# High rows of a feed-forward product eight steps behind its low rows, and a new order in VectorE's list of deferred work

## The chip, the core and the metric

The kernel runs on one core of one Trainium2 chip. Its engines are TensorE (PE in the profile; PEld is its loading of weights), VectorE (DVE), ScalarE (ACT), GpSimd (POOL) and SyncE (SP), which here only issues transfers. Each works through its own row of instructions in the order of the program, and they wait for each other by semaphores. The metric is the time of one execution in microseconds (us); lower is better.

## The reference

The input x has 2048 rows of 512 values in float32. Two branches are computed from it and mixed by a gate of one number for each row.

```python
g = _sigmoid((x * gate_w).sum(-1, keepdims=True))
# a: 32 query heads of 16 columns, one key and one value head for all of them
q = (x @ wq).reshape(B, S, H, Dh).transpose(0, 2, 1, 3); k = x @ wk; v = x @ wv
p = _softmax(jnp.einsum("bhqd,bkd->bhqk", q, k) * Dh ** -0.5, axis=-1)
a = jnp.einsum("bhqk,bkd->bhqd", p, v).transpose(0, 2, 1, 3).reshape(B, S, 512) @ wo
# b: a feed-forward product with 1792 hidden columns
b = (_silu(x @ w_gate) * (x @ w_up)) @ w_down
return g * a + (1 - g) * b
```

## The kernel before

**Two kinds of work share TensorE.** Attention is cut into units: one head and 128 keys. A unit's scores for all 2048 queries fill two tiles `pss` of 128x1024 (L658), ScalarE turns them into `pt` by an exponential (L666), and four matmuls multiply `pt` by the values into `po` (L678, "the mix"; a block's four units make sixteen, which the profile counts as 32). The feed-forward work is a list of jobs. A gate job or an up job multiplies one chunk of 512 rows of x with 128 columns of `w_gate` or `w_up` in 12 matmuls; a down job multiplies finished hidden columns with `w_down` in 12 or 15. Every operand is kept as a high and a low float32r part (`xh`, `xl`), and three products of the parts stand for one.

**Blocks.** After a beginning, the loop runs blocks of four units (`block`, L709). A block's order is the string `STEPS`: eight S, each one score tile, and sixteen F, each one step of feed-forward work; then the mix of four units. I call the time from the start of one block's mix to the start of the next one's a period.

**Low and high rows.** TensorE takes a feed-forward matmul as two halves of 64 rows that run side by side. In a step, `Halves.step` (L377) issues one matmul of the low rows of one job and one of the high rows of another, older one. The high rows of a job may begin when `LAG` counts have passed since its low rows ended; a step counts 1, a score tile 1 and the mix 16. VectorE's one-element memset `sign` (L401) stands between the two halves of a job as a tick. Both halves add up in one bank of PSUM, and there are three such banks (`ps_f`, tiles `pf`). When the high rows end, VectorE empties the bank (`EVAC`): `hs<-pf` (L265) for a gate, the product `ht<-ht,pf` (L292) or `ht<-hs,pf` (L294) for an up, `acc` (L327, L329) for a down. `SLACK = 7` counts later the bank counts as free and the next low rows may be placed in it; on the chip their first matmul waits for that copy. Where a score tile that VectorE must help with follows within two places, the emptying is held back until that tile has been issued (`HOLD`), so it stands behind VectorE's copy `pt<-pss` (L662): for three tiles of a block VectorE copies one half of the scores out, and ScalarE works on that half in place later.

**VectorE's deferred list.** The gate needs silu, built from a tanh on ScalarE (L274, issued at the end of the block, behind its exponentials) and VectorE's `ht<-ht,hs` (L282, "the gate's product"). L282 goes into the list `DEFER`; so does, once the up job has ended, the pair that splits the finished hidden column, `hh<-ht` (L106) and `hl<-ht,hh` (L107), "the casts". If an up job ends before its L282 has been issued, `up` issues it on the spot, straight ahead of L292. If an up job ends in the same block as its gate, ahead of the tanh, the kernel multiplies first (L294), runs the tanh in place (L278) and defers L296 instead of L282. A second list, `LATER`, holds the six pieces of the normalization of a finished head: a shuffle (L696), four reciprocals (L687) and a product with its stores (L690), "the norms". At the end of a block, L740 to L745 issue up to two norms and then entries of `DEFER`, each with a cost, until the budget of 3.2 is used up or the head of the list doesn't fit. The mix is issued behind that and keeps TensorE busy meanwhile.

**The end.** Jobs that don't fit into the blocks are done with all 128 rows behind the last mix (`whole`, L355), and then the attention's output product (`finish`). GpSimd splits the weights (L106, L107 with `wgh`, `wdl` and so on) in that part as everywhere.

Of the kernel before, what the change touches and what calls it, by code (L numbers as in the profile page):

```python
# [36 lines left out]
ORDER = (0, 1, 2, 3)  # L37
GROUPS = ((0, 1, 2, 3, 4), (5, 6, 7, 8, 9), (10, 11, 12, 13))
SLACK = 7
LAG = 6  # L40
LONG = 8
GAP = 36
WARM = 30
# [19 lines left out]
def tile_gated_mix(ctx, tc, x, wq, wk, wv, wo, w_gate, w_up, w_down, gate_w, out):  # L63
# [41 lines left out]
    def split(hi, lo, src, eng=nc.gpsimd, eng_hi=nc.vector):  # L105
        eng_hi.tensor_copy(hi, src)  # L106
        eng.tensor_tensor(lo, src, hi.bitcast(F32), ALU.subtract)  # L107


    def three(a, b, sa, sb):  # L110
        return [(a[0][sa], b[0][sb]), (a[0][sa], b[1][sb]), (a[1][sa], b[0][sb])]
# [10 lines left out]
    ACTS, DEFER, LOADS, HOLD, EVAC = [], [], [], [], []  # L122

    def run(queue, n):
        for _ in range(min(n, len(queue))):
            queue.pop(0)()
# [16 lines left out]
    def load_w(nm, n):  # L143
        if n < NCH * NF:
            fs = slice(n % NF * P, (n % NF + 1) * P)
            if nm == "d":
                W[nm, n] = load_split(w_down[fs, :], "wd", 5)
            else:
                W[nm, n] = load_split({"g": wg_v, "u": wu_v}[nm][:, :, fs], "w" + nm, 2)
# [102 lines left out]
    def gate_up(n, c):  # L252
        t = []

        def project(nm):
            def terms():
                r = []
                for k in range(KD):
                    r += three(W[nm, n], XC[c], (slice(None), k), (slice(None), k))
                return r  # L260
            return terms

        def gate(ps):
            g = wp.tile([P, CH], F32, name="hs", bufs=2)
            nc.vector.tensor_copy(g, ps)  # L265

            t.append(wp.tile([P, CH], F32, name="ht", bufs=2))

            t.append(g)
            assert n < 2 or n - 2 in HT  # L270

            def tanh():
                if len(t) == 2:
                    nc.scalar.activation(t[0], g, AF.Tanh, scale=0.5)  # L274
                    DEFER.append((0.7, silu))
                    t.append(silu)
                else:
                    nc.scalar.activation(g, g, AF.Tanh, scale=0.5)  # L278

            def silu():  # L280
                if len(t) == 3:
                    nc.vector.scalar_tensor_tensor(t[0], t[0], 1.0, g, op0=ALU.add, op1=ALU.mult)  # L282
                    t.append(None)

            ACTS.append(tanh)

        def up(ps):
            hh = wp.tile([P, CH], F32R, name="hh", bufs=7)
            hl = wp.tile([P, CH], F32R, name="hl", bufs=7)
            if len(t) > 2:  # L290
                t[2]()
                nc.vector.tensor_tensor(t[0], t[0], ps, ALU.mult)  # L292
            else:
                nc.vector.tensor_tensor(t[0], t[1], ps, ALU.mult)  # L294
                t.append(lambda: None)
                DEFER.append((0.7, lambda: nc.vector.scalar_tensor_tensor(t[0], t[1], 1.0, t[0], op0=ALU.add, op1=ALU.mult)))  # L296

            def cast():
                split(hh, hl, t[0], nc.vector)
                HT[n] = (hh, hl)  # L300

            DEFER.append((1.2, cast))

        r = []
        for nm, end in (("g", gate), ("u", up)):
            r.append(Job(3 * KD, lambda nm=nm: (nm, n) in W and c in XC, project(nm), end))
            r[-1].after.append(lambda nm=nm: load_w(nm, n + 2))
        return r
# [67 lines left out]
    class Halves:  # L376
# [6 lines left out]
        def step(self, more):  # L383
# [3 lines left out]
            if not self.low and more and JOBS and JOBS[0].ready() and self.free and min(self.free) <= self.clock:  # L387
                self.free.remove(min(self.free))
                self.low = [JOBS.pop(0), 0]
            if not self.high and self.wait and self.wait[0][1] + LAG <= self.clock:  # L390
                self.high = [self.wait.pop(0)[0], 0]
# [241 lines left out]
    PO, LATER = [], []  # L633
    hp = tc.alloc_tile_pool(name="hp", bufs=2)
    with tc.tile_pool(name="bpool", bufs=2) as bp:
# [29 lines left out]
        def exps(pt, ps, other=None, w=slice(None)):  # L665
            ins = nc.scalar.activation(pt[:, w], ps[:, w], AF.Exp, scale=SCALE)  # L666
            if other is not None:
                tc.declare_no_dep(getattr(ins, "ins", ins), getattr(other, "ins", other), reason="another bank")

        def mix(u):  # L670
            h, kt = divmod(u, NT)
            pt = PT.pop(u)
            if kt == 0:
                run(COPY, 1)
                PO[:] = [ps_o.tile([P, CH], F32, name="po")]
            po = PO[0]
            for c in range(NCH):
                nc.tensor.matmul(po[c * 2 * DH:(c + 1) * 2 * DH, :], vaug[:, kt, :], pt[:, c * CH:(c + 1) * CH],  # L678
                                 start=(kt == 0), stop=(kt == NT - 1))
            if kt == NT - 1:  # L680

                osb = hp.tile([P, CH], F32, name="osb")
                rsb = hp.tile([P, CH], F32, name="rsb", bufs=1)

                def invert(i):
                    w = slice(i * P, (i + 1) * P)
                    nc.vector.reciprocal(rsb[:, w], rsb[:, w])  # L687

                def store():
                    nc.vector.tensor_tensor(osb, osb, rsb, ALU.mult)  # L690
                    for c in range(NCH):
                        nc.sync.dma_start(o_d[h * DH:(h + 1) * DH, c * CH:(c + 1) * CH],
                                          osb[c * 2 * DH:c * 2 * DH + DH, :])

                COPY.append(lambda: nc.vector.tensor_copy(osb, po))
                LATER.extend([(0.8, lambda: nc.vector.stream_shuffle(rsb, osb, [DH] * 2 * DH))] +  # L696
                             [(1.0, lambda i=i: invert(i)) for i in range(TC)] + [(0.8, store)])
# [5 lines left out]
        def feed(k, more=True):  # L703
            for _ in range(k):
                if JOBS and more or halves.busy():
                    halves.step(more)

        def block(k, first, last, steps, kinds, order):
            more = k < NB - STOP  # L709
            tiles = [(u, j) for u in range(first, last) for j in range(2)]  # L710
            order = list(order)
            made = []

            def emit():
                while order and order[0] != "|" and int(order[0][0]) < len(made):
                    i, how = int(order[0][0]), order.pop(0)[1]
                    pt, ps, other = made[i]
                    if how == "s":
                        exps(pt, pt, w=slice(CH, None))
                    else:  # L720
                        exps(pt, ps, other, slice(0, CH) if kinds[i] == "H" else slice(None))

            for i, what in enumerate(steps):
                if what == "F":
                    if "S" in steps[i + 1:i + 3] and kinds[len(made):len(made) + 1] == "H":
                        HOLD.append(i)
                    feed(1, more)
                    HOLD.clear()
                elif len(made) < len(tiles):
                    made.append(score(*tiles[len(made)], kinds[len(made)] == "H"))  # L730
                    emit()
                    run(EVAC, len(EVAC))
                if len(made) > 4:
                    run(COPY, 1)
            if order:
                order.pop(0)
            run(ACTS, len(ACTS))
            emit()
            assert not order and len(made) == len(tiles)
            left = BUDGET  # L740
            for queue, n in ((LATER, 2), (DEFER, len(DEFER))):
                while n and queue and queue[0][0] <= left:
                    cost, f = queue.pop(0)
                    left, n = left - cost, n - 1
                    f()  # L745
            for u in range(BLOCK * k, BLOCK * (k + 1)):
                mix(u)
            halves.clock += 2 * LONG
# [7 lines left out]
        with tc.manual_schedule():  # L756
# [25 lines left out]
            for k in range(2 * BEGIN // BLOCK, NB):  # L782
                u = BLOCK * k
                if k == 2 * BEGIN // BLOCK:
                    n = u + 6 - (u + 1)
# [129 lines left out]
```

## Time and profile before

| | |
|---|---|
| median of three runs | 1369.03 us (1368.62 to 1370.0) |
| the profiled execution, its own time | 1366.99 us |
| its span, from the first to the last instruction | 1364.9 us |
| granted TensorE clock, mean | 0.999 |
| busy share: TensorE, VectorE, ScalarE, GpSimd | 98%, 53%, 78%, 29% |

In the views quoted below, a row of a timeline gives the start in the span, the time, engine, line and operation, and in brackets how long the engine had been idle and what ended that. A row of the waits gives who waited for whom, total us, number and longest. A row of windows gives the stretch, its length, and the busy us of PE, PEld, DVE, ACT and POOL with instructions in brackets, the granted clock and the transfers. TensorE's busy share hides short waits, since matmuls overlap; the lengths of the periods don't.

### The profile page before, as it was taken

The numbers are of one execution on the slowest core, as the hardware profiler recorded it, in microseconds if no ns is written. First come the engines' busy times: TensorE is split into PE (matmuls) and PEld (weight loads), VectorE is DVE, ScalarE is ACT, GpSimd is POOL, SyncE is SP. The second block draws the span as 40 slices with busy tenths as digits, with TensorE's granted clock in tenths as the row PEclk, the third lists the DMA queues.
The fourth block names the chain that finished last, engine by engine and source line by source line (L and its number), as shares of the span: only waits on it lengthen the run. The fifth ranks groups of instructions, "written<-read, shape, count | busy, mean of one in ns | idle before, by whom it ended". The sixth has DMA issues, their size and how long they took to land. (4 is left out here: it accounts for less than half of the span.)

```text
span 1364.9 us, 26750 instructions
## 1 busy us (share of the span) xinstructions
PE 1332.3 (98%) x10755; PEld 767.4 (56%) x10755; DVE 722.6 (53%) x1222; ACT 1061.2 (78%) x1463; POOL 390.6 (29%) x408
## 2 busy tenths in 40 slices
PE   9999999999999999999999999999999999999997
PEld 7654555555555555555555555555555555555576
DVE  5554555455545456556455555456464566465432
ACT  4578888888888888888888888888888888888500
POOL 6140321052221232232041151232131331053353
PEclk9999999999999999999999999999999999999999
DMA  8455311131241221121151130231221221132154
GB/s 273 144 178 193 81 43 29 27 102 43 62 125 36 80 78 34 53 68 51 36 144 36 60 95 25 59 82 36 59 69 34 89 66 34 35 96 59 36 166 141
DMA packets 101489, 107.79 MB, mean 79 GB/s; under 512 B 9968, under 2 KB 69616, under 8 KB 99696
## 3 DMA queue, kind: packets, MB, share of 16 engines
q1 hardware_dynamic: 99632, 105.81, 27.0%
q8 instruction: 88, 1.44, 0.5%
q10 hardware_dynamic: 1728, 0.20, 0.1%
q14 instruction: 41, 0.34, 0.1%
HBM read 76.09 MB, written 29.36 MB: 77 GB/s over the span
## 5 line engine op out<-in xcount | busy, mean ns | idle before, releaser
L666 ACT ACTIVATE pt<-pss 128x1024 f32<-128x1024 f32 (+1 forms) x1024 | 841.1, 875 | 200.7 <-PE pss L658 170.4
L678 PE MATMUL po<-pt,vaug 128*32 128x512 f32 x4096 | 467.6, 595 | 0.0
L662 DVE COPY pt<-pss 128x512 f32<-128x512 f32 x354 | 244.6, 692 | 372.4 <-PE pss L658 332.8
L658 PE MATMUL pss<-qs,ks 64*128 64x512 f32 x2048 | 397.2, 415 | 2.0 <-ACT pt L666 1.1
L658 PEld LDWEIGHTS pss<-qs,ks 64*128 64x128 f32 x2048 | 192.4, 184 | 215.4 <-ACT pt L666 133.7
L678 PEld LDWEIGHTS po<-pt,vaug 128*32 128x32 f32 x4096 | 119.2, 109 | 261.5 <-issue 255.8
L666 ACT ACTIVATE pt<-pt 128x512 f32<-128x512 f32 x354 | 195.7, 620 | 0.0
L175 PE MATMUL pf<-xh,wgh 64*128 64x512 f32 (+1 forms) x444 | 165.7, 393 | 8.4 <-DVE sign L401 7.8
L175 PE MATMUL pf<-xh,wuh 64*128 64x512 f32 (+1 forms) x440 | 163.6, 393 | 4.0 <-DVE sign L401 3.2
L175 PE MATMUL pf<-xh,wgl 64*128 64x512 f32 (+1 forms) x444 | 165.5, 394 | 0.0
L175 PE MATMUL pf<-xl,wgh 64*128 64x512 f32 (+1 forms) x444 | 165.4, 390 | 0.0
L175 PE MATMUL pf<-xh,wul 64*128 64x512 f32 (+1 forms) x440 | 163.8, 394 | 0.0
L175 PE MATMUL pf<-wdh,hh 64*128 64x512 f32 (+1 forms) x427 | 154.6, 392 | 5.4 <-DVE sign L401 5.1
L175 PE MATMUL pf<-xl,wuh 64*128 64x512 f32 (+1 forms) x440 | 159.8, 390 | 0.0
L175 PE MATMUL pf<-wdl,hh 64*128 64x512 f32 (+1 forms) x427 | 153.5, 391 | 2.5 <-POOL wdl L107 2.5
L175 PE MATMUL pf<-wdh,hl 64*128 64x512 f32 (+1 forms) x427 | 155.7, 392 | 0.0
L106 POOL CAST wgh<-wraw 128x512 fp32r<-128x512 f32 x56 | 35.5, 634 | 402.6 <-PE pf L175 321.0
L106 POOL CAST wuh<-wraw 128x512 fp32r<-128x512 f32 x56 | 35.5, 634 | 323.4 <-PE pf L175 284.1
L687 DVE RECIPROCAL rsb<-rsb 128x128 f32<-128x128 f32 x128 | 117.0, 935 | 6.2 <-issue 4.5
L175 PEld LDWEIGHTS pf<-xh,wgh 64*128 64x128 f32 (+1 forms) x444 | 80.3, 185 | 19.5 <-issue 9.2
L175 PEld LDWEIGHTS pf<-xh,wuh 64*128 64x128 f32 (+1 forms) x440 | 79.6, 185 | 15.3 <-issue 6.2
L175 PEld LDWEIGHTS pf<-wdh,hh 64*128 64x128 f32 (+1 forms) x427 | 78.4, 185 | 15.7 <-DVE sign L401 7.5
(157 smaller groups left out, 1580.3 us busy)
## 6 DMA issues: line engine op xcount, KB each, us to landing
wraw<-in_B_w_gate_dram SPq DMA_DIRECT2D x56, 256.0 KB
wraw<-in_B_w_up_dram SPq DMA_DIRECT2D x56, 256.0 KB
wraw<-in_B_w_down_dram SPq DMA_DIRECT2D x56, 256.0 KB
qs<-q_d SPq DMA_DIRECT2D x62, 192.0 KB
q_d<-hl SPq DMA_DIRECT2D x18, 256.0 KB
q_d<-hh SPq DMA_DIRECT2D x18, 256.0 KB
o_d<-osb SPq DMA_DIRECT2D x128, 32.0 KB
a_d<-acc SPq DMA_DIRECT2D x4, 1024.0 KB
```

The source lines that it names most:

```text
L106: eng_hi.tensor_copy(hi, src)
L175: ins = nc.tensor.matmul(self.ps, a, b, start=(i == 0 and not half), stop=(last and half != 0))
L658: nc.tensor.matmul(ps[:, b * CH:(b + 1) * CH], ks[rows, kt * P:(kt + 1) * P], QS[h][rows, j, :], start=True, stop=True)
L662: other = nc.vector.tensor_copy(pt[:, CH:], ps[:, CH:]) if half else None
L666: ins = nc.scalar.activation(pt[:, w], ps[:, w], AF.Exp, scale=SCALE)
L678: nc.tensor.matmul(po[c * 2 * DH:(c + 1) * 2 * DH, :], vaug[:, kt, :], pt[:, c * CH:(c + 1) * CH], start=(kt == 0), stop=(kt == NT - 1))
L687: nc.vector.reciprocal(rsb[:, w], rsb[:, w])
```

## The change

`LAG` goes from 6 to 8, so the high rows of a job begin two counts later. The gate's product L282 goes to the head of `DEFER` and no longer to its end, so it stands ahead of the casts of the job before. With two or more entries in `DEFER`, a block issues one norm and not two. An assertion checks that `LATER` is empty when a new head's norms are added; it adds no instruction. From L695 on, line numbers grow by one.

```diff
-LAG = 6
+LAG = 8
...
                     nc.scalar.activation(t[0], g, AF.Tanh, scale=0.5)
-                    DEFER.append((0.7, silu))
+                    DEFER.insert(0, (0.7, silu))
...
+                assert not LATER
                 COPY.append(lambda: nc.vector.tensor_copy(osb, po))
...
             left = BUDGET
-            for queue, n in ((LATER, 2), (DEFER, len(DEFER))):
+            for queue, n in ((LATER, 1 if len(DEFER) > 1 else 2), (DEFER, len(DEFER))):
                 while n and queue and queue[0][0] <= left:
                     cost, f = queue.pop(0)
                     left, n = left - cost, n - 1
                     f()
```

Two places show what moves. The first is VectorE's row around one gate and its up job, from the emptying of the gate's bank (`hs<-pf`) to the tick behind the up job's product (`ht<-ht,pf`); `rsb` belongs to the norms, `pt<-pss` is the copy of scores. Before, about 617 to 626 us into the span:

```order
L265 COPY hs<-pf 128x512
L687 RECIPROCAL rsb<-rsb 128x128 x2
L106 CAST hh<-ht 128x512
L107 TENSOR_TENSOR hl<-ht,hh 128x512
L662 COPY pt<-pss 128x512
L401 MEMSET sign 1x1
L662 COPY pt<-pss 128x512 x2
L282 SCALAR_TENSOR_TENSOR ht<-ht,hs 128x512
L292 TENSOR_TENSOR ht<-ht,pf 128x512
L401 MEMSET sign 1x1
```

The same gate and up job in the changed kernel:

```order
L265 COPY hs<-pf 128x512
L687 RECIPROCAL rsb<-rsb 128x128
L282 SCALAR_TENSOR_TENSOR ht<-ht,hs 128x512
L106 CAST hh<-ht 128x512
L107 TENSOR_TENSOR hl<-ht,hh 128x512
L662 COPY pt<-pss 128x512
L401 MEMSET sign 1x1
L662 COPY pt<-pss 128x512 x2
L292 TENSOR_TENSOR ht<-ht,pf 128x512
L401 MEMSET sign 1x1
```

The gate's product has moved from directly ahead of L292, behind two copies of scores, to the end of the block before, ahead of the casts and of the next block's first copy.

The second place is TensorE's row in a block, with tile numbers: each `pf` number is one job in one bank. Before, in the same block, from the first high row of a new job (`pf_6978`) to the first low row of the next one (`pf_7126`), which takes the bank of `pf_6884`; that one's last high row stands two rows ahead of this piece, and its emptying is held back behind the score tile in the second row:

```order
L175 MATMUL pf_6978<-xh_230,wuh_6860 128x512
L658 MATMUL pss_7096<-qs_6482,ks_78 128x512 x2
L175 MATMUL pf_7068<-xh_230,wgl_6912 128x512
L175 MATMUL pf_6978<-xl_231,wuh_6860 128x512
L175 MATMUL pf_7068<-xh_230,wgh_6911 128x512
L175 MATMUL pf_6978<-xh_230,wul_6861 128x512
L658 MATMUL pss_7114<-qs_6482,ks_78 128x512 x2
L175 MATMUL pf_7068<-xl_231,wgh_6911 128x512
L175 MATMUL pf_6978<-xh_230,wuh_6860 128x512
L175 MATMUL pf_7068<-xh_230,wgl_6912 128x512
L175 MATMUL pf_6978<-xl_231,wuh_6860 128x512
L175 MATMUL pf_7126<-xh_230,wuh_7016 128x512
```

A block of the changed kernel, from the row behind the last high row of `pf_7707`; its emptying is issued at once, ahead of the score tile in the first row:

```order
L658 MATMUL pss_7942<-qs_7370,ks_78 128x512 x2
L175 MATMUL pf_7902<-xh_230,wuh_7392 128x512
L175 MATMUL pf_7801<-xh_230,wgh_7294 128x512
L175 MATMUL pf_7902<-xl_231,wuh_7392 128x512
L175 MATMUL pf_7801<-xl_231,wgh_7294 128x512
L175 MATMUL pf_7902<-xh_230,wul_7393 128x512
L175 MATMUL pf_7801<-xh_230,wgl_7295 128x512
L658 MATMUL pss_7953<-qs_7370,ks_78 128x512 x2
L175 MATMUL pf_7902<-xh_230,wuh_7392 128x512
L175 MATMUL pf_7801<-xh_230,wgh_7294 128x512
L175 MATMUL pf_7902<-xl_231,wuh_7392 128x512
L175 MATMUL pf_7801<-xl_231,wgh_7294 128x512
```

The first low row in `pf_7707`'s bank comes another score tile and two rows later. From a bank's last high row to its next user there were five steps and two score tiles; here there are six and three, and the copy is not held back. Of the emptyings in the 118 blocks ahead of the last one, 61 of 149 were held back before, and 28 of 148 are now.

## Prediction

> **What bounds the kernel now.** I read the page first, then who waits on TensorE, then windows of one period each, then the timeline of single waits.
>
> ```profile
> span 1364.9 us, 26750 instructions
> PE 1332.3 (98%) x10755; PEld 767.4 (56%) x10755; DVE 722.6 (53%) x1222; ACT 1061.2 (78%) x1463; POOL 390.6 (29%) x408
> ```
>
> TensorE is busy for 98%, so only its waits and its number of steps can move the time. Who waits on TensorE:
>
> ```profile
> engine line waited for: us in total, times, longest us
> PE pf L175 <- DVE sign L401: 16.1, 22, 1.8
> PE pf L175 <- POOL wdl L107: 2.5, 2, 1.4
> PE pss L658 <- ACT pt L666: 1.1, 2, 0.9
> ...
> PE pf L175 <- POOL wgl L107: 0.2, 1, 0.2
> ```
>
> That names VectorE, but overlapping matmuls hide part of each wait. The lengths of the periods hide nothing. I cut the 118 periods from 137.33 to 1275.11 us into four groups by what stands in the order, and asked for each group's windows: 78 quiet ones, 29 with an ordinary emptying late for the next low rows, 8 in which an up job had to issue its gate's product (L282) on the spot just ahead of a bank's next user, and 3 behind a block that ended with tanh, product and casts. One quiet, one late and one on-the-spot period stand first, then the sums in that order; the three of the last group stand with theirs.
>
> ```profile
> core 0: us, PE busy (x) PEld busy (x) DVE busy (x) ACT busy (x) POOL busy (x), PEclk, DMA share, GB/s
> 597.69:607.05 9.36, 9.36 (x82) 5.12 (x80) 6.05 (x12) 8.45 (x14) 2.98 (x4) 1.00 0.10 30
> 607.05:617.09 10.04, 9.64 (x82) 5.23 (x81) 6.41 (x11) 8.59 (x14) 2.49 (x3) 1.00 0.00 1
> 617.09:628.62 11.53, 9.73 (x83) 5.46 (x81) 5.78 (x10) 7.78 (x12) 2.45 (x3) 1.00 0.42 111
> ...
> sum 732.83, PE 732.83 PEld 411.57 DVE 398.64 ACT 628.92 POOL 171.83; mean PE 9.40 PEld 5.28 DVE 5.11 ACT 8.06 POOL 2.20
> ...
> sum 286.28, PE 279.94 PEld 153.84 DVE 144.94 ACT 235.53 POOL 92.61; mean PE 9.65 PEld 5.30 DVE 5.00 ACT 8.12 POOL 3.19
> ...
> sum 89.00, PE 77.52 PEld 42.60 DVE 57.56 ACT 72.97 POOL 32.00; mean PE 9.69 PEld 5.33 DVE 7.20 ACT 9.12 POOL 4.00
> ...
> 393.83:403.57 9.74, 9.60 (x82) 5.45 (x80) 5.55 (x12) 8.54 (x14) 2.19 (x4) 1.00 0.93 292
> 511.81:521.55 9.74, 9.59 (x82) 5.33 (x80) 7.60 (x14) 8.55 (x14) 2.96 (x4) 1.00 0.34 76
> 898.05:908.24 10.19, 9.62 (x82) 5.38 (x80) 5.66 (x12) 8.55 (x14) 4.79 (x5) 1.00 0.55 130
> sum 29.67, PE 28.82 PEld 16.16 DVE 18.82 ACT 25.64 POOL 9.94; mean PE 9.61 PEld 5.39 DVE 6.27 ACT 8.55 POOL 3.31
> ```
>
> A quiet period takes 732.83 / 78 = 9.395 us, TensorE busy throughout. Over that, the 29 lose 286.28 - 272.46 = 13.8 us, the 8 lose 89.00 - 75.16 = 13.8, the 3 lose 29.67 - 28.19 = 1.5: 29.1 us of waits, all there is to win in the blocks.
>
> One on-the-spot wait, in the third window, with VectorE, GpSimd and the matmul that waited:
>
> ```profile
> 622.92 0.69 DVE L662 COPY pt<-pss 128x512 f32<-128x512 f32 x1 [0.69 <-PE pss L658]
> 623.53 1.71 DVE L282 SCALAR_TENSOR_TENSOR ht<-ht,hs 128x512 f32<-128x512 f32 x1
> 625.27 0.69 DVE L292 TENSOR_TENSOR ht<-ht,pf 128x512 f32<-128x512 f32 x1
> ...
> 623.41 1.28 POOL L107 TENSOR_TENSOR wul<-wraw,wuh 128x512 fp32r<-128x512 f32 x1
> ...
> 626.10 0.46 PE L175 MATMUL pf<-xh,wgh 64*128 64x512 f32 x1 [1.80 <-DVE sign L401]
> ```
>
> The view names the tick, which ends at the same moment; but a tick's own job begins its high rows counts later, while the matmul at 626.10 is the first low row of a new job in the bank that L292 has just emptied. So the waits are for emptied banks, and they end when copy, product and emptying have run one behind the other.
>
> **The change, part by part.** LAG first. A job's high rows, and so its last one, stand two counts later against the low rows. That changes where the emptying falls in `STEPS`: the second pair of TensorE's rows shows six steps and three tiles where there were five and two, and no hold. In the changed order I counted the places of the late kind, an emptying held behind VectorE's copy with no more than five steps and one tile, or four and two, until the next user: ten are left. Four places of that kind in the trace of before:
>
> ```profile
> sum 39.24, PE 38.66 PEld 21.34 DVE 21.82 ACT 33.12 POOL 9.33; mean PE 9.66 PEld 5.33 DVE 5.46 ACT 8.28 POOL 2.33
> ```
>
> 39.24 / 4 - 9.395 = 0.42 us each, so 10 x 0.42 = 4.2 us stay of 13.8; bounds 0 (no wait is left) and 13.8 (LAG changes nothing).
>
> The gate's product at the head of the list, and one norm instead of two. The first pair of orders shows it: no up job issues L282 on the spot any more (13 did, 8 of them in the way). The 13.8 us go. The product costs the same 0.69 us in its new place, under the mix; but it waits there for the tanh, and the casts that used to fill that wait now come behind it, ahead of the next block's first score copy. Blocks that end so were 3 and are 19. One of the three, from ScalarE's tanh to the score tile that needs VectorE's copy out of the way (L296 stands where L282 will):
>
> ```profile
> 514.59 0.64 ACT L278 ACTIVATE hs<-hs 128x512 f32<-128x512 f32 x1
> ...
> 515.25 0.69 DVE L296 SCALAR_TENSOR_TENSOR ht<-hs,ht 128x512 f32<-128x512 f32 x1 [1.03 <-ACT hs L278]
> 515.98 0.43 DVE L106 CAST hh<-ht 128x512 fp32r<-128x512 f32 x1
> 516.44 0.69 DVE L107 TENSOR_TENSOR hl<-ht,hh 128x512 fp32r<-128x512 f32 x1
> 517.05 1.29 DVE L662 COPY pt<-pss 128x512 f32<-128x512 f32 x2
> ...
> 517.88 0.50 PE L658 MATMUL pss<-qs,ks 64*128 64x512 f32 x2
> ```
>
> The chain runs without a gap to 517.7, when the first copy is out, and the tile starts at 517.88. Its price is in the three windows: 9.74 or 10.19 less 9.395, 0.35 to 0.80 us, mean 0.50. I take the mean, 19 x 0.50 = 9.4 us (6.6 to 15.1). Queued behind the waiting product on VectorE are the casts (a down job reads the newest column last, nine or twelve steps in), the copy, for which TensorE waits as priced, and the tick, whose reader is counts away; ScalarE's half in place comes four tiles later.
>
> The norms are the same instructions in other blocks: 25 blocks issue one now (1 before), 76 two (88 before), 17 none (29 before).
>
> ```profile
> L687 DVE RECIPROCAL rsb<-rsb 128x128 f32<-128x128 f32 x128 | 117.0, 935 | 6.2 <-issue 4.5 <-DVE pt L662 0.4 <-DVE ht L292 0.2
> ...
> 617.09 3.64 PE L678 MATMUL po<-pt,vaug 128*32 128x512 f32 x32
> ```
>
> One takes 0.94 us and lies under 3.64 us of mix, ahead of a product that waits for its tanh anyway: 0 us. Without that cover, the 12 blocks that have a norm and had none would pay 12 x 0.94 = 11.2. A gain is not to be had, since the tanh sets the time. A head's stores follow up to two blocks later in SP's row; the output part reads them.
>
> The loads of the next weights hang on a job's end, so SP issues them, and GpSimd splits them, two counts later. The first view has 0.2 us of waits for such a split, and a weight is needed two jobs later: 0 us, at most two steps (0.5 us) for each of the few that were close. The assertion issues nothing.
>
> Steps and the end. By the counter that the kernel prints as it is built, the loop makes 2048 steps instead of 2051, of which 70 instead of 52 positions are empty on one side; one job more (12 full matmuls, 111 instead of 99) runs behind the last mix.
>
> ```profile
> 1299.02 0.39 PE L175 MATMUL pf<-wdl,hh 128*128 128x512 f32 x1
> 1299.24 0.39 PE L175 MATMUL pf<-wdh,hl 128*128 128x512 f32 x1
> ...
> 1301.46 0.50 PE L175 MATMUL pf<-wdl,hh 128*128 128x512 f32 x1 [1.37 <-POOL wdl L107]
> ...
> 1303.88 0.50 PE L175 MATMUL pf<-wdl,hh 128*128 128x512 f32 x1 [1.17 <-POOL wdl L107]
> ```
>
> A full matmul follows the other after 0.22 to 0.23 us, so the job takes 2.7 us and three steps give 0.7. But TensorE then waits 1.37 + 1.17 = 2.5 us for GpSimd's splits of `w_down`, whose row starts with the last mix and doesn't move; the job fits into that wait. I take 2.7 - 2.5 = 0.2; bounds 0 and 2.7.
>
> **The sum**, against the profiled execution's 1366.99 us (2.1 more than its span): waits 29.1 to 4.2 + 9.4 = 13.6, a gain of 15.5; steps gain 0.7; the job costs 0.2. 1366.99 - 16.0 = 1351.0. The median of the runs is 2.0 higher, so 1353.0 us.
>
> **The rivals.** One: LAG doesn't move the waits, because the bank is emptied later as well. Then 13.8 stay and the sum gains 29.1 - 13.8 - 9.4 + 0.5 = 6.4: 1362.6. For it: high and low rows shift against each other, and a wait can move to the next bank. Against it: the order has 28 held emptyings where there were 61.
>
> Two, on the other side: GpSimd stretches the new chain.
>
> ```profile
> L106 DVE CAST hh<-ht x56: 361/418/1507, 137.9 to 1300.9; 128x512 fp32r<-128x512 f32 x56
> L282 DVE SCALAR_TENSOR_TENSOR ht<-ht,hs x51: 691/693/1709, 128.4 to 1298.0; 128x512 f32<-128x512 f32 x51
> ```
>
> A cast takes 0.42 us at the median and up to 1.51; the product above took 1.71 instead of 0.69, started 0.12 us after a split on GpSimd and ended 0.55 after it. Now both stand in a chain that TensorE waits for. Were every chain stretched by 1.71 - 0.69 = 1.02, the 19 would cost 19 x 1.52 = 28.9, and the sum is 28.9 + 4.2 - 29.1 - 0.5 = 3.5 more: 1372.5. It decides from (29.1 + 0.5 - 4.2) / 19 = 1.34 us a chain. For it: of the three windows the one with 4.79 us of GpSimd is the slow one. Against it: GpSimd is busy for 29%, its splits start when a job ends and are mostly done when the tanh is, and two of three chains ran clean. The Trainium skill (SBUF — State Buffer, section "Who interferes with whom") says that VectorE and GpSimd share one pair of ports as an exclusive lock, so that a cast, or an operation with two inputs in SBUF, is blocked for all of the other's instruction. By that rule, if a split stood in each chain's way, the time would be this rival's 1372.5, against 1353.0 by the three windows. The trace agrees that the delay is a whole instruction (1.02 us), not a share.
>
> Three: nothing waits, since the new chains also hide: 29.1 + 0.7 - 0.2 = 29.6 less, 1339.4. Against it: three of three chains cost something.
>
> **Chances.** The sum 0.70; rival one 0.12; two 0.10; three 0.05; something slower that I don't see 0.03. The likeliest time is 1353.0. All chains at 0.35 and no late emptying give 1346, rival one 1363; 1345 to 1363 leaves out rivals two and three and some edge. Within 0.2%, about 2.7 us, this kernel can't be told from the one before. Faster: the sum, rivals one and three, less 0.02 for rival one's upper edge, 0.85. Same: that edge and 0.03 of rival two, 0.05. Slower: the rest, 0.10.
>
> **What would show it.** In the profile after: L282 no longer idles directly ahead of L292, and waits of TensorE for the tick fall from 16.1 to some 3 to 6 us; score tiles (L658) wait for VectorE some 19 times, 0.3 to 0.8 us each, in blocks behind a tanh; a quiet period is 9.4 as before; the wait for `wdl` behind the last mix shrinks below 0.5. I'm wrong if periods of 10 us and more stay frequent: with L282 or a cast of over 1 us ahead, it is rival two; with a copy held behind a score tile, rival one.

## The result, and the profile after

The changed kernel takes 1356.02 us (1354.04 to 1357.41), the kernel before 1369.01 in the same series: a ratio of 0.9903, with a 95% interval of 0.9886 to 0.992. It is faster by 13.0 us, where 16.0 were forecast. The profiled execution took 1354.91 us, 12.1 less than the one before, with a span of 1352.7.

Who waits on TensorE in the changed kernel (total us, number, longest):

```profile
engine line waited for: us in total, times, longest us
PE pss L658 <- DVE sign L401: 6.6, 8, 1.9
PE pf L175 <- DVE hh L106: 1.7, 1, 1.7
PE pss L658 <- ACT pt L666: 1.6, 3, 0.9
PE pf L175 <- DVE sign L401: 0.5, 3, 0.2
PE pf L175 <- POOL wdl L107: 0.2, 1, 0.2
```

The waits for emptied banks (`pf` for the tick) are nearly gone, 16.1 to 0.5 us. New are waits of score tiles (`pss`) for VectorE, 6.6 us where that row had 0.6. The wait for `wdl` behind the last mix fell from 2.5 to 0.2, and a wait of 1.7 for VectorE's cast `hh` has come up there.

The lengths of the periods between 137.33 and 1263.05 us tell more, since overlap hides nothing there. First come the sums of 94 quiet periods and of 5 with a held emptying; then, of the 19 periods behind a block that ends with tanh, product and casts, the sum of 14, and the other five singly with their sum:

```profile
core 0: us, PE busy (x) PEld busy (x) DVE busy (x) ACT busy (x) POOL busy (x), PEclk, DMA share, GB/s
sum 883.87, PE 883.50 PEld 494.91 DVE 472.26 ACT 757.33 POOL 216.60; mean PE 9.40 PEld 5.27 DVE 5.02 ACT 8.06 POOL 2.30
...
sum 48.99, PE 48.16 PEld 26.24 DVE 27.04 ACT 42.41 POOL 16.70; mean PE 9.63 PEld 5.25 DVE 5.41 ACT 8.48 POOL 3.34
...
sum 136.78, PE 135.26 PEld 74.97 DVE 79.65 ACT 120.63 POOL 35.03; mean PE 9.66 PEld 5.35 DVE 5.69 ACT 8.62 POOL 2.50
...
288.80:301.84 13.04, 11.14 (x82) 6.84 (x80) 7.59 (x12) 9.49 (x15) 7.38 (x7) 0.87 0.52 140
585.79:596.35 10.56, 9.88 (x83) 5.32 (x81) 6.03 (x12) 8.92 (x14) 8.69 (x10) 1.00 0.41 110
785.02:795.98 10.96, 9.60 (x82) 5.41 (x80) 6.41 (x11) 8.54 (x14) 6.10 (x7) 1.00 0.47 122
995.25:1005.76 10.51, 9.60 (x82) 5.42 (x80) 6.44 (x12) 8.54 (x14) 5.59 (x6) 1.00 0.17 51
1081.09:1092.10 11.01, 9.60 (x82) 5.34 (x80) 6.63 (x13) 8.56 (x14) 9.18 (x9) 1.00 0.39 111
sum 56.08, PE 49.83 PEld 28.33 DVE 33.10 ACT 44.05 POOL 36.94; mean PE 9.97 PEld 5.67 DVE 6.62 ACT 8.81 POOL 7.39
```

A quiet period takes 883.87 / 94 = 9.403 us. Over that, the 5 held ones lose 2.0, the 14 chains 5.1 (0.37 each) and the five chains 9.1 (1.8 each). The five stand out by the last of the busy columns: GpSimd works 5.6 to 9.2 us in them, against a mean of 2.5 in the 14. From the end of the tanh to the end of the casts GpSimd works in all five; of the 14 it does so in one (405.80 to 415.84), where it makes VectorE's subtraction 0.40 us longer.

Inside the last of the five, the chain from ScalarE's tanh to the score tile that waits:

```profile
1083.87 0.64 ACT L274 ACTIVATE ht<-hs 128x512 f32<-128x512 f32 x1
1084.53 0.69 DVE L282 SCALAR_TENSOR_TENSOR ht<-ht,hs 128x512 f32<-128x512 f32 x1 [3.34 <-ACT ht L274]
1085.02 0.68 POOL L106 CAST wdh<-wraw 128x512 fp32r<-128x512 f32 x1 [0.61 <-DMA wraw<-in_B_w_down_dram]
1085.14 0.83 DVE L106 CAST hh<-ht 128x512 fp32r<-128x512 f32 x1
1085.78 1.35 POOL L107 TENSOR_TENSOR wdl<-wraw,wdh 128x512 fp32r<-128x512 f32 x1
1086.01 1.66 DVE L107 TENSOR_TENSOR hl<-ht,hh 128x512 fp32r<-128x512 f32 x1
1087.60 1.29 DVE L662 COPY pt<-pss 128x512 f32<-128x512 f32 x2
...
1088.42 0.50 PE L658 MATMUL pss<-qs,ks 64*128 64x512 f32 x2 [1.41 <-DVE sign L401]
```

VectorE's subtraction starts 0.23 us after GpSimd's and ends 0.54 after it: 1.66 us instead of 0.69. The cast took 0.83 instead of 0.42. Product, casts and copy stand in one row without a gap, so each delay reaches the score tile.

### The profile page after: what moved, and what is told of

It reads as the page before. It is cut to its first block, busy times and chain, and to the rows that moved or that the text cites. A ratio compares the mean times of both kernels' runs of the same rounds, so it can differ in the third digit from the quotient of the medians.

```text
span 1352.7 us, 26754 instructions
## 1 busy us (share of the span) xinstructions
PE 1330.9 (98%) x10743; PEld 769.5 (57%) x10743; DVE 715.2 (53%) x1221; ACT 1062.6 (79%) x1463; POOL 388.8 (29%) x408
## 5 line engine op out<-in xcount | busy, mean ns | idle before, releaser
L658 PE MATMUL pss<-qs,ks 64*128 64x512 f32 x2048 | 401.3, 417 | 9.1 <-DVE sign L401 6.6
L175 PE MATMUL pf<-xh,wgh 64*128 64x512 f32 (+1 forms) x440 | 160.8, 392 | 0.5 <-DVE sign L401 0.2
L175 PE MATMUL pf<-xl,wgh 64*128 64x512 f32 (+1 forms) x440 | 160.7, 391 | 0.0
L175 PE MATMUL pf<-xh,wuh 64*128 64x512 f32 (+1 forms) x440 | 159.4, 393 | 0.5 <-DVE sign L401 0.3
L175 PE MATMUL pf<-xh,wul 64*128 64x512 f32 (+1 forms) x440 | 158.6, 393 | 0.0
L175 PE MATMUL pf<-wdh,hh 64*128 64x512 f32 (+1 forms) x427 | 143.4, 391 | 1.7 <-DVE hh L106 1.7
L175 PE MATMUL pf<-wdh,hl 64*128 64x512 f32 (+1 forms) x427 | 144.1, 390 | 0.0
L175 PE MATMUL pf<-wdl,hh 64*128 64x512 f32 (+1 forms) x427 | 143.5, 390 | 0.0
L282 DVE SCALAR_TENSOR_TENSOR ht<-ht,hs 128x512 f32<-128x512 f32 x48 | 36.2, 753 | 122.0 <-ACT ht L274 122.0
```

What stands on the lines that cost most here:

```text
L175: ins = nc.tensor.matmul(self.ps, a, b, start=(i == 0 and not half), stop=(last and half != 0))
L658: nc.tensor.matmul(ps[:, b * CH:(b + 1) * CH], ks[rows, kt * P:(kt + 1) * P], QS[h][rows, j, :], start=True, stop=True)
```

## The experiments

The two parts of the change were first tried apart on the kernel before.

**LAG alone.**

```diff
-LAG = 6
+LAG = 8
```

> The kernel before with LAG = 8 alone; the deferred list and the norms stay as they were. By the program 28 emptyings of 148 are held instead of 61 of 149, the gate's product is asked for on the spot in 12 blocks, in 8 of them just ahead of a bank's next user (before: 13 and 8), and 5 blocks end with tanh, product, casts (before: 3). Main theory (a wait belongs either to a late emptying or to a chain on VectorE, and the two parts of the change act apart): late emptyings fall from 13.8 to about 4 us, the products on the spot stay at 13.8, five chains at 0.75 give 3.8, the three steps fewer give 0.7 and the end loses 0.5: 21.6 instead of 29.1 us of waits, so 7 to 8 us less than before, about 1361. Rival one (late emptyings were not caused by the distance): within 1 us of before, 1368 to 1370. Rival of the other sort (the distance alone is the whole gain, the lists give nothing): 1356.

Measured: 1353.3 us (1352.66 to 1354.04) against 1368.76, ratio 0.9887 (0.9871 to 0.9902). That is 15.5 us less (13.1 between the profiled executions), not 7 to 8. In its profile the sums are those of the 8 periods with a product on the spot in the way, of 5 chains and of 7 with a late emptying:

```profile
sum 86.15, PE 77.86 PEld 42.96 DVE 56.72 ACT 73.08 POOL 26.53; mean PE 9.73 PEld 5.37 DVE 7.09 ACT 9.13 POOL 3.32
...
sum 49.00, PE 48.29 PEld 26.89 DVE 30.03 ACT 43.00 POOL 14.46; mean PE 9.66 PEld 5.38 DVE 6.01 ACT 8.60 POOL 2.89
...
sum 68.59, PE 67.57 PEld 36.69 DVE 38.67 ACT 59.73 POOL 23.90; mean PE 9.65 PEld 5.24 DVE 5.52 ACT 8.53 POOL 3.41
```

Less 9.395 a period they lose 11.0, 2.0 and 2.8: 15.8 us of waits instead of 29.1. The expectation had 13.8, 3.8 and 4. Late emptyings went as forecast; the products on the spot became a little cheaper, and these chains met little of GpSimd. LAG alone and the whole change can't be told apart by their times (the intervals overlap), so the two list edits together added nothing that shows, though they took away its 8 products on the spot.

**The two list edits alone** (LAG stays 6).

```diff
-                    DEFER.append((0.7, silu))
+                    DEFER.insert(0, (0.7, silu))
...
-            for queue, n in ((LATER, 2), (DEFER, len(DEFER))):
+            for queue, n in ((LATER, 1 if len(DEFER) > 1 else 2), (DEFER, len(DEFER))):
```

> The kernel before with LAG = 6 and the two edits of the lists (the gate's product at the head, one norm instead of two where two or more entries are deferred). No product is asked for on the spot any more (13 before), 41 emptyings of 149 are held (61 before), and 21 blocks end with tanh, product, casts. Main theory: products on the spot 13.8 to 0, late emptyings 13.8 to about 9, chains 21 at the 0.75 us measured in the changed kernel give 15.7 instead of 1.5: 25 instead of 29 us of waits, so some 4 us less, about 1365. Rival (the lists are the whole gain and the distance gives nothing): 1356. Second rival (chains cost 1.8 us each wherever GpSimd is at work, and more of them meet it here): 1370 or above.

Measured: 1361.98 us (1360.48 to 1362.55), ratio 0.9946 (0.9932 to 0.996): 6.8 us less, near the expected 4. The 21 periods behind its chains:

```profile
sum 212.77, PE 204.80 PEld 114.78 DVE 124.60 ACT 179.94 POOL 87.91; mean PE 9.75 PEld 5.47 DVE 5.93 ACT 8.57 POOL 4.19
```

212.77 - 21 x 9.395 = 15.5 us, or 0.74 a chain: the price of the changed kernel, 14.2 / 19 = 0.75, comes again in another order of work. Both sums hold one period of about 13 us with a low clock (the last section). The theory that the two parts of the change act apart doesn't hold: alone they gave 15.5 and 6.8 us, together 13.0.

**The limit of norms alone** (LAG 6, the product still behind the casts).

```diff
-            for queue, n in ((LATER, 2), (DEFER, len(DEFER))):
+            for queue, n in ((LATER, 1 if len(DEFER) > 1 else 2), (DEFER, len(DEFER))):
```

> The kernel before with one edit alone: one norm instead of two where two or more entries are deferred. LAG stays 6 and the gate's product stays behind the casts. No product is asked for on the spot, 41 emptyings of 149 are held, and 5 blocks end with tanh, product, casts (the kernel with both list edits: none, 41 and 21). Main theory (the head of the list only makes chains, the limit of norms alone removes the products on the spot): 16 chains fewer than with both list edits at 0.6 to 0.75 us, so 9.6 to 12 us below its 1362.0, 1350 to 1352.5. Rival (the head of the list is what removes the waits at the banks, the limit does little): near the kernel before, 1366 to 1369. Second rival (distance and lists simply add up, as if the head cost nothing here): 1362.

Measured: 1351.91 us (1350.21 to 1356.48, a wide spread) against 1368.94, ratio 0.9887 (0.9868 to 0.9906). One norm fewer at the end of a block, by itself, takes 17 us away. The products on the spot are gone without the head of the list; with one norm (1.0) the budget of 3.2 has room for casts (1.2) and product (0.7), with two it hadn't. The head added to this costs 1361.98 - 1351.91 = 10.1 us; the two kernels were measured in different series, whose kernels before agree within 0.2 us.

**The change with the product back behind the casts** (LAG 8 and the limit).

```diff
-                    DEFER.insert(0, (0.7, silu))
+                    DEFER.append((0.7, silu))
```

> The changed kernel with one edit taken back: the gate's product is appended behind the casts again instead of put at the head; LAG = 8 and the limit of one norm stay. No product is asked for on the spot, 28 emptyings of 148 are held as in the changed kernel, but the casts now stand ahead of the product and so run while ScalarE still computes the tanh: 8 blocks end with tanh, product, casts instead of 19. Main theory (the loss against the forecast is the price of the 19 chains, 14.2 us): 11 chains fewer at 0.75 give 8 us less than the changed kernel, 1347 to 1349. Rival (the first score tiles wait for the tanh and the product, whatever the casts do): 1355 to 1357, as the changed kernel.

Measured: 1346.55 us (1345.3 to 1348.5), ratio 0.984 (0.9826 to 0.9853), 9.5 less than the changed kernel. The same five periods as above:

```profile
289.12:300.58 11.46, 9.86 (x82) 5.32 (x81) 7.27 (x12) 8.92 (x14) 7.04 (x7) 1.00 0.52 132
583.37:593.08 9.71, 9.60 (x82) 5.08 (x81) 5.28 (x11) 8.81 (x14) 7.23 (x8) 1.00 0.37 102
781.66:792.49 10.83, 9.61 (x82) 5.44 (x81) 6.29 (x11) 8.55 (x14) 6.04 (x6) 1.00 0.55 123
991.64:1001.04 9.40, 9.40 (x83) 5.48 (x81) 6.73 (x12) 8.45 (x14) 6.87 (x6) 1.00 0.19 56
1076.13:1085.51 9.38, 9.38 (x83) 5.26 (x81) 6.70 (x13) 8.46 (x14) 8.16 (x8) 1.00 0.31 93
```

GpSimd is about as busy as before: 6.0 to 8.2 us. In the second, fourth and fifth the casts now run while ScalarE computes the tanh, and these periods fall from 10.56, 10.51 and 11.01 to 9.71, 9.40 and 9.38. VectorE is still held in the last two, by a subtraction of 1.65 and a cast of 1.38 us, but both end ahead of the tanh:

```profile
992.92 1.65 DVE L107 TENSOR_TENSOR hl<-ht,hh 128x512 fp32r<-128x512 f32 x1
995.10 0.69 DVE L282 SCALAR_TENSOR_TENSOR ht<-ht,hs 128x512 f32<-128x512 f32 x1 [0.52 <-ACT ht L274]
...
1076.15 1.38 DVE L106 CAST hh<-ht 128x512 fp32r<-128x512 f32 x1
...
1079.57 0.69 DVE L282 SCALAR_TENSOR_TENSOR ht<-ht,hs 128x512 f32<-128x512 f32 x1 [1.03 <-ACT ht L274]
```

In the first and third the block ends with L296, which the casts need and so must follow; they stay long. So in these five, GpSimd's work costs time where the casts stand between the tanh and the score copy, and not where they stand ahead of the tanh.

**No subtraction on GpSimd.** The low parts of the feed-forward weights are zeros, so the kernel leaves them out of its products.

```diff
+    ZERO = wp.tile([P, CH], F32R, name="zero", bufs=1)
+    nc.gpsimd.memset(ZERO.bitcast(F32), 0.0)
...
+        if name in ("wg", "wu", "wd"):
+            nc.gpsimd.tensor_copy(hi, raw)
+            return hi, (ZERO if name == "wd" else ZERO.rearrange("p (k f) -> p k f", f=P))
         lo = pool.tile(shape, F32R, name=name + "l", bufs=bufs)
```

> The changed kernel without GpSimd's subtraction for the feed-forward weights: their low parts are one tile of zeros, written once, so the low parts of w_gate, w_up and w_down are left out of the computation; casts, loads, TensorE's steps and VectorE's work stay. GpSimd's 168 subtractions of 1.3 us vanish, 219 us of its work. Main theory (five of the 19 chains were stretched because GpSimd's work on the weights stood beside them: 9.1 us over the quiet period together, against 0.35 for each of the other 14): most of the five fall to 0.35 to 0.7, so 5.5 to 7.5 us less than the changed kernel, 1348.5 to 1350.5, and the cast of the high part and the subtraction on VectorE (mean 499 and 803 ns in the changed kernel) become shorter, about 420 and 720 ns. Rival (the stretch comes from the loads' traffic or from VectorE's own list, not from GpSimd): within 1 us of the changed kernel, with the same five long periods.

Measured: 1346.33 us (1345.17 to 1346.58), ratio 0.9835 (0.9821 to 0.9848), 9.7 less than the changed kernel. VectorE's casts fell to a mean of 415 ns and its subtractions to 697. The five periods:

```profile
sum 49.76, PE 48.52 PEld 26.88 DVE 28.09 ACT 43.43 POOL 8.73; mean PE 9.71 PEld 5.38 DVE 5.62 ACT 8.69 POOL 1.75
```

They lose 49.76 - 47.0 = 2.7 us instead of 9.1. The rival (the loads' traffic, or VectorE's own list) falls: loads and list were all still there. Of the 8.1 us between the two profiles' spans, 6.4 lie in the five periods; behind the last mix 2.5 more were saved (80.18 us to the end instead of 82.65), and the beginning took 1.0 longer.

**Copies on GpSimd instead of the subtraction.** The kernel leaves out the subtraction, so its low parts are not those of the product; it shows a time alone.

```diff
+        if name in ("wg", "wu", "wd"):
+            nc.gpsimd.tensor_copy(hi, raw)
+            lo = pool.tile(shape, F32R, name=name + "l", bufs=bufs)
+            for _ in range(2):
+                nc.gpsimd.tensor_copy(lo, raw)
+            return hi, lo
```

> The changed kernel in which GpSimd writes the low parts of the feed-forward weights by two copies of the raw tile (one input, about 0.61 us each) instead of one subtraction (two inputs, 1.30 us): the computation has wrong low parts there, GpSimd is as busy as in the changed kernel and at the same places. Theory A (VectorE is held only while GpSimd runs the subtraction with two inputs; its copies do not hold it): the five long periods after a chain become short, 1346 to 1349, as with the low parts left out, and VectorE's casts and subtractions keep 0.42 and 0.70 us beside a busy GpSimd. Theory B (any work of GpSimd holds VectorE): 1354 to 1357, as the changed kernel, with VectorE's casts at 0.8 and its subtractions at 1.2 us where GpSimd runs.

Measured: 1348.84 us (1348.52 to 1350.09), ratio 0.9855 (0.984 to 0.987). The time is the one theory A gave, but its reason is wrong. The five periods lose only 4.4 us over five quiet ones, while GpSimd works 31 us in them instead of 37:

```profile
sum 51.42, PE 48.55 PEld 26.71 DVE 33.42 ACT 43.41 POOL 30.95; mean PE 9.71 PEld 5.34 DVE 6.68 ACT 8.68 POOL 6.19
```

VectorE's cast and subtraction in the whole run (least, median and longest in ns):

```profile
L106 DVE CAST hh<-ht x56: 361/420/837, 139.6 to 1287.3; 128x512 fp32r<-128x512 f32 x56
L107 DVE TENSOR_TENSOR hl<-ht,hh x56: 691/693/1071, 140.3 to 1287.7; 128x512 fp32r<-128x512 f32 x56
```

In the changed kernel:

```profile
L106 DVE CAST hh<-ht x56: 361/420/1505, 137.9 to 1291.4; 128x512 fp32r<-128x512 f32 x56
L107 DVE TENSOR_TENSOR hl<-ht,hh x56: 691/692/1664, 138.3 to 1291.8; 128x512 fp32r<-128x512 f32 x56
```

Copies do hold VectorE, so it is not the subtraction alone. The hold is shorter because the instruction is: in both runs a held operation ends a fixed time after GpSimd's instruction, whichever that is (the last section).

**The subtraction in halves.**

```diff
-        split(hi, lo, raw, nc.gpsimd, nc.gpsimd)
+        nc.gpsimd.tensor_copy(hi, raw)
+        m = shape[1] // 2
+        for w in (slice(0, m), slice(m, 2 * m)):
+            nc.gpsimd.tensor_tensor(lo[:, w], raw[:, w], hi[:, w].bitcast(F32), ALU.subtract)
```

> The changed kernel with GpSimd's subtraction of 128x512 (1.30 us) cut into two of half the columns, some 0.65 us each: the same work, nothing left out, GpSimd as busy as before. Theory (VectorE is held to the end of the one GpSimd instruction that runs, so the length of an instruction decides): VectorE's longest subtraction falls from 1.66 to about 1.1 us and its longest cast from 1.5 to about 0.85, as with the two copies, and the time comes near that run's 1348.8: 1348.5 to 1352. Rival (GpSimd's second half follows at once and takes the place of the first, so a chain is held as long as with one instruction): 1354 to 1357, with the long rows as they were.

Measured: 1350.16 us (1349.08 to 1351.81), ratio 0.9858 (0.9837 to 0.988), 5.9 less than the changed kernel. The five periods' sum:

```profile
sum 53.23, PE 48.55 PEld 27.04 DVE 35.23 ACT 43.50 POOL 36.67; mean PE 9.71 PEld 5.41 DVE 7.05 ACT 8.70 POOL 7.33
```

VectorE's cast and subtraction:

```profile
L106 DVE CAST hh<-ht x56: 362/420/956, 139.5 to 1288.1; 128x512 fp32r<-128x512 f32 x56
L107 DVE TENSOR_TENSOR hl<-ht,hh x56: 691/693/1114, 139.9 to 1288.9; 128x512 fp32r<-128x512 f32 x56
```

The longest holds shrank as expected, and so far the theory stands. But the five periods fell only from 56.08 to 53.23, most of it in the first one, where the clock had been low; a chain of cast and subtraction can meet two holds. Of the 5.9 us the profiles show 3.0 (spans of 1352.7 and 1349.7). How much the length of a single GpSimd instruction is worth stays open.

**Two steps further.** First `LAG = 5` with the limit and the product behind the casts, since that order holds fewer emptyings:

```diff
-LAG = 8
+LAG = 5
```

> The kernel with LAG = 8 and the limit of one norm, product behind the casts (1346.6), with LAG = 5 instead of 8: 17 emptyings of 149 are held instead of 28 of 148, 8 blocks end with tanh, product, casts as there, and Halves takes 2044 steps instead of 2048 (4 x 0.23 = 0.9 us). If the waits are late emptyings and chains: 1343 to 1346. If eight steps of distance had a worth of their own beyond the number of held emptyings: 1349 or more.

Measured: 1343.19 us (1342.86 to 1344.06), ratio 0.9817 (0.9803 to 0.983). So a distance of eight has no worth of its own. That the fewer held emptyings give the rest fits the expected time, but no run shows their part alone. Then the casts are kept from behind a fresh product:

```diff
+            fresh = len(ACTS) > 0
             run(ACTS, len(ACTS))
...
-                while n and queue and queue[0][0] <= left:
+                after = False
+                while n and queue and queue[0][0] <= left and not (after and queue[0][0] == 1.2):
                     cost, f = queue.pop(0)
+                    after = after or queue is DEFER and cost == 0.7 and fresh
```

> The same with LAG = 5 and one rule more: at the end of a block that issued a tanh, a pair of casts behind a product waits for the next block, so that no block ends with tanh, product, casts any more (8 before). If the chain's price is the casts behind the product: 8 chains go, some 0.5 us each, 1339 to 1343. If it is the product itself, or if the postponed casts are missed later by the jobs that need them: no less than the kernel beside it, 1344 to 1347.

Measured: 1338.48 us (1337.43 to 1338.98), ratio 0.978 (0.9766 to 0.9793), 17.5 us less than the changed kernel and the fastest here. The sum of 117 periods of this kernel, all but the last two:

```profile
sum 1099.27, PE 1099.09 PEld 614.81 DVE 613.65 ACT 954.56 POOL 305.86; mean PE 9.39 PEld 5.25 DVE 5.24 ACT 8.16 POOL 2.61
```

1099.27 / 117 = 9.395 us: all of them together are as long as quiet ones, and TensorE is busy throughout. The first row of who waits on TensorE now lies behind the last mix:

```profile
PE pf L175 <- POOL wdl L107: 2.5, 2, 1.4
```

With GpSimd's halves added:

> The kernel with LAG = 5, the product behind the casts, the limit of one norm and no casts behind a fresh product (1338.5), with GpSimd's subtractions cut in halves as beside it. Since no block ends with tanh, product, casts any more, shorter holds have little left to shorten: 1336 to 1339. If the halves cost GpSimd more time than they give back, the wait of TensorE for the low part of w_down (2.5 us in two waits) grows: 1339 to 1342.

Measured: 1340.37 us (1340.23 to 1340.47), ratio 0.979 (0.9772 to 0.9808): nothing gained. The halves take 0.75 to 0.79 us each in the mean, not 0.65, and the wait for `wdl` stayed at 2.5.

## Why the prediction was right, and where it was not

**The direction and most of the size** were right: 1356.02 lies 3.0 above the forecast and inside the range. In the profiles the gain is 12.1 us where 16.0 were forecast.

**What bounds the kernel.** The split of 29.1 us of waits by period held. A quiet period is 9.403 after 9.395, and the kernel in which nothing is left to wait comes to 1338.48, close to the 1339.4 that the third rival worked out from that split (though with another `LAG` and so not quite the same steps).

**LAG.** Forecast 4.2 us left of 13.8. The five held periods lose 2.0, or 0.40 each where 0.42 was taken; the other five of the ten fall into chain periods, where the price can't be taken apart. With LAG alone, 2.8 are left. Rival one falls.

**The products on the spot.** All 13 vanished, as forecast. The step named head and limit together and counted the norms as 0; the runs show that the limit alone does it, and that the head only costs time here. That was not asked in the prediction, though the order of the work could have shown it.

**The new chains.** This is the step that failed in size: "I take the mean, 19 x 0.50 = 9.4 us (6.6 to 15.1)". The 19 blocks are the ones that were counted, but they cost 14.2 us, 4.8 more. The 14 clean ones cost 0.37, as the lower of the two prices had it; five cost 1.8. Behind the 0.50 stood the argument against rival two, that GpSimd's splits "are mostly done when the tanh is". In 13 of 19 no GpSimd instruction runs in the chain, and in a 14th the hold is 0.40. In the other five rival two's mechanism is at work, and nearly at its price. Four of them cost (43.04 - 4 x 9.403) / 4 = 1.36 us, 0.99 more than a clean chain, where the rival had 1.02 more; product and casts there took 0.57, 1.22, 0.89 and 1.39 us longer than their medians. That the rival's price fits the mean is partly luck, since a hold can have any length up to GpSimd's instruction. The first of the five was held for 1.75 and cost 3.64, because the clock fell as well. The rival doesn't decide: the mean of 0.75 stays below the 1.34 from which it would.

**Steps and the end.** The period ahead of the last mix went from 7.69 to 7.00 us, the forecast 0.7. From the last mix to the end it grew from 82.10 to 82.65, 0.55 instead of 0.2; the wait for `wdl` shrank to 0.2 as said. But the prediction has no term for the wait that came up in its place, for the casts of a column that is finished there:

```profile
1291.95 0.47 PE L175 MATMUL pf<-wdh,hh 128*128 128x512 f32 x1 [1.67 <-DVE hh L106]
```

The job of 2.7, 2.3 less for `wdl` and 1.7 for `hh` would make 2.1; the other 1.5 were won in rows that nobody took apart. So this term came near by luck.

**The sum.** Forecast waits of 13.6; measured 14.2 + 2.0, and 0.9 because a quiet period, the measure for all 118, is 0.008 us longer: 17.1. With 0.35 more at the end, that is the 3.9 us by which the profiled gain falls short. The held emptyings, 2.2 below their term, made up for part of the chains, 4.8 above theirs.

## What to carry to other kernels

Work that needs a result of another engine should stand behind independent work in its engine's row: the casts filled the wait for the tanh for nothing, and put behind it they cost 9.5 to 10.1 us in two pairs of runs. When two edits are meant for one wait, count in the order of the work which of them removes it; here the smaller one did, and the other one only cost time. A price taken from three places is a price for those three places: look at what else ran beside them before it is multiplied.

## What the runs showed of the hardware

**GpSimd holds VectorE.** VectorE's casts, and its operations with two inputs in SBUF, stretch when they meet a GpSimd instruction: the subtraction took up to 1.66 us beside GpSimd's subtraction of 1.35 and 1.07 beside its copies of 0.61. The product L292, with one input in PSUM, never took over 0.69 in the changed kernel, and the reciprocals, with one input in SBUF, stayed within 0.96:

```profile
L687 DVE RECIPROCAL rsb<-rsb x128: 893/946/955, 94.2 to 1285.7; 128x128 f32<-128x128 f32 x128
```

The Trainium skill (SBUF — State Buffer, section "SBUF: two separate sides") has the pair of ports as a lock that whoever starts first keeps for the whole instruction. The traces agree. In all twelve together, 302 of the casts, subtractions and products of VectorE's two lists were stretched by more than 0.3 us; every cast among them ends 0.28 to 0.29 us after the end of a GpSimd instruction and every other one 0.54 to 0.55, whether that instruction is a subtraction, a half of one or a copy. So the hold is what is left of GpSimd's instruction when VectorE's starts. The 1.02 us that the prediction calls a whole instruction came from the rest of one of 1.28, 0.12 us into it.

**The granted clock fell after a wait of 1.90 us.** In the first of the five periods a score tile waited:

```profile
296.62 0.50 PE L658 MATMUL pss<-qs,ks 64*128 64x512 f32 x2 [1.90 <-DVE sign L401]
```

Then the clock was at half for 3.41 us (the third column from the end of each window):

```profile
294.37:297.79 3.42, 1.52 (x14) 1.13 (x12) 2.71 (x4) 1.29 (x3) 1.10 (x2) 1.00 0.68 181
297.79:301.20 3.41, 3.41 (x19) 2.96 (x18) 1.78 (x4) 2.69 (x5) 1.75 (x2) 0.50 0.08 18
301.20:304.61 3.41, 3.41 (x34) 1.20 (x36) 1.46 (x3) 3.19 (x5) 0.00 (x0) 1.00 0.22 64
```

That is why a period with one wait of 1.90 us was 3.64 longer: half of 3.41 us, where TensorE had work throughout, makes 1.7, an estimate. With the list edits alone a wait of 1.91 us did the same (a mean of 0.58 over the next 3 us). The wait of 1.80 us that the prediction quotes was followed by 1.00. The length of a wait gives no clean threshold: behind the last mix, one wait of 2.00 us (the limit of norms alone) was followed by 1.00 and one of 1.69 (limit and `LAG` = 8) by 0.59.

Where the wait falls matters too. In all twelve traces the times from one change of the clock to the next are whole multiples of 3.413 us (1 to 398 of them). Cut into such stretches, the one ahead of the fall held 1.90 us without TensorE, 1.91 with the list edits alone and 1.69 behind the limit with `LAG` = 8. The wait of 2.00 us lay across two stretches, with 1.25 and 1.60 us idle, and the one of 1.80 had 1.30 in its first. Even so it isn't clean: a stretch with 1.52 us idle was followed by 1.00 in the kernel before (731.43 to 734.84), and one with 1.47 by 0.50 in the fastest kernel (1270.96 to 1274.37). The Trainium skill (TensorE: Matmul & The Clock Gate, section "HAM oscillation — how this bites in real kernels") speaks of idle gaps over some 3.4 us; here shorter ones were enough, and no run was made to find what else has to come together.
